# A planned single-core kernel: recurrence, routing and expert tiles, with a new plan, Newton norms and fillers of ones

## The chip, the cores and the metric

The kernel runs on one core of a Trainium2 chip. The metric is the device time of the whole kernel in microseconds, the median over timed runs; the three runs shown of the kernel before have the median 506.29 us (505.67 to 507.88).

## The reference

```python
# x, f_logit: (4, 5056, 256); expert_emb: (8, 256); w1: (8, 256, 1024); w2: (8, 1024, 256)
f = lower_bound + (1 - lower_bound) * sigmoid(f_logit)
for t in range(5056):                       # recurrence along the sequence
    h = f[:, t] * h + (1 - f[:, t]) * x[:, t];  y[:, t] = h
x = y.reshape(20224, 256)
logits = (x / (norm(x) + 1e-6)) @ (expert_emb / (norm(expert_emb) + 1e-6)).T / tau
e = argmax(logits);  gate = softmax(logits)[e]
out = gate * (relu(x @ w1[e]) @ w2[e])      # each token by its one expert
```

## The kernel before

The tokens come in 40 chunks of 512 (the last has 256). For each chunk SyncE loads `f_logit` and `x` (three buffers each); TensorE transposes both (L667, L701); ScalarE makes the gate by tanh (L678, L684); VectorE makes the input term (L709) and runs the recurrence as a scan (L725). ScalarE squares the result (L737). For the first 12 chunks TensorE transposes the result back and ScalarE stores it into `Yt` (L761, L772), later ones go through a bf16 copy and a transposing DMA of SyncE (L743, L748). Two chunks make a group: TensorE computes logits and norms (L819, L823) and ranks the tokens within each expert by triangular matmuls (L887 to L900); some forty short VectorE steps give slot, gate and row. GpSimd then scatters the group's rows, 128 at a time, to the slots of a scratch table in DRAM (`XsScratch`, L1015, 158 scatters).

A tile is 256 slots of one expert. SyncE loads its rows transposed (`ys`, L1207) and its gates and row numbers (`xm`, L1212). TensorE runs 16 matmuls of the first layer (L1247); ScalarE and VectorE evict them by relu into `hT` (L1265, L1270, two buffers). TensorE runs 16 matmuls of the second layer in four steps of four (L1284); ScalarE evicts the first 128 tokens with the gate as scale (L1299), VectorE the others (L1303), into `osb` (four buffers), and GpSimd scatters each half to `out` (L1309, 166 scatters). 83 tiles run here; three more can be needed by the data and are skipped ("late" tiles). All 16 weight arrays are loaded by GpSimd with a cast to bf16 (L647), two at a time, and every tile waits for all of them. A table that `update_` writes after some groups tells which rows a tile reads, so tiles can begin before the last chunk is routed.

What sets the order on each queue is a planner. Each operation is recorded with engine, cost, priority (the chunk number; 10000 + j for tile j; -1 for evictions of tiles and for output scatters), what it reads and writes. `schedule` simulates the five queues with these costs and places, on the engine that can start first, the ready operation of the lowest priority number; banks of PSUM are handed out in the same way (kind "a" for chunks, "m" and "o" for the layers of a tile). The result is a fixed order for each in-order queue, and semaphores carry the dependencies. Two constants tell how scatters and TensorE meet: an end of a TensorE step is planned no earlier than 2500 ns after the start of the last scatter (`SHADOW`), and each scatter waits for the latest TensorE step planned to end 900 ns before the scatter's start (`PACE`), which makes it follow TensorE on the chip too:

```python
if e == "pe": o.end = max(o.end, scat + self.SHADOW)
...
past = [q for t, q in steps[-40:] if t <= s - self.PACE and (o.late or not q.late)]
if past: o.deps.append(past[-1])
```

Of the kernel before, what the change touches and what calls it, by code (L numbers as in the profile page):

```python
# [34 lines left out]
class Prog:  # L35
# [8 lines left out]
    SHADOW = 2500  # L44
    DMA_FIX = 1900
    PACE = 900.0
    DMA_RATE = 400.0

# [65 lines left out]

    def schedule(self, first, caps):
# [24 lines left out]
        bus, scat = 0.0, -1e9  # L140
# [7 lines left out]
        def lag(d):  # L148
            return d.end + self.LAT[d.eng] + self.PAD

# [5 lines left out]
        while True:  # L156
# [16 lines left out]
            if avail[e]:  # L173
                p, i, o = heapq.heappop(avail[e])
            else:
                t, p, i, o = heapq.heappop(wait[e])
            new = [h for h in o.hold if h.b is None]
# [19 lines left out]
            if o.dma is not None:  # L197
                bus = max(bus, free[e]) + o.nbytes / self.DMA_RATE
                o.end = max(bus, free[e]) + self.DMA_FIX
            else:  # L200
                o.end = free[e] + self.LAG[e]
                if e == "pe":
                    o.end = max(o.end, scat + self.SHADOW)
            if e == "pe" and not o.quiet:
                steps.append((free[e], o))
            if e == "pool" and o.dma is not None:
                scat = s
# [121 lines left out]
def bass_hgrn_recurrence__then__cosine_router_kernel(  # L329
# [38 lines left out]
    with ExitStack() as es:  # L368
# [79 lines left out]
        NO = 4  # L448
# [3 lines left out]


        def pool(fn, cost=400, **k):
            return op("pool", fn, cost, **k)
# [12 lines left out]


# [21 lines left out]

        load(0)
        sp(lambda e: e.dma_start(embt[:], moe_expert_emb[:]), 8192, "ld0", w=["embt"])
# [13 lines left out]
        def iota(dst, pattern, base=0, mult=0, w=()):  # L507
# [3 lines left out]

        pool(lambda e: e.memset(ident[:], 0.0), w=["ident"])
# [10 lines left out]
            2, r=["lb0", "lb1"], w=["cs0"],  # L523
# [3 lines left out]
            2, r=["lb0", "lb1"], w=["cs1"],  # L527
# [13 lines left out]
        pool(lambda e: e.memset(onesb[:], 1.0), w=["onesb"])  # L541
# [10 lines left out]
        def late_constants():  # L552
# [54 lines left out]
        dve(lambda e: e.tensor_tensor(ew(3), ew(0), ew(2), ALU.mult), 1, r=["ew0", "ew2"], w=["ew3"])  # L607
        dve(lambda e: e.tensor_tensor(ew(4), ew(1), ew(3), ALU.add), 1, r=["ew1", "ew3"], w=["ew4"])
        dve(
            lambda e: e.tensor_scalar(ew(5), ew(4), 0.5, 1e-6, op0=ALU.mult, op1=ALU.add),  # L610
            1, r=["ew4"], w=["ew5"],
        )
# [20 lines left out]
        )  # L633


        def wload(i, c):
# [9 lines left out]
            op(  # L646
                "pool", lambda e: e.dma_start(dst, src), 1000, w=[("w", i)], dma=f"w{i}",  # L647
                deps=[pr.writer.get(("w", i - 2))], nbytes=1 << 20, prio=c,
            )
# [82 lines left out]
        def Y_(c):  # L732
# [8 lines left out]
            if c >= CT and nb == 4:  # L741
                act(
                    lambda e: e.activation(hbf[c % NHF][:], hb[c % NH][:], AF.Copy),  # L743
                    2 * n, r=[("hb", c % NH, 0), ("hb", c % NH, 1)], w=[("hbf", c % NHF)],
                )
                for dh in range(DT):
                    sp(
                        lambda e, dh=dh: e.dma_start_transpose(  # L748
                            Yt[y][:, gi * 8 + k_ * 4 : gi * 8 + k_ * 4 + 4, dh * P : (dh + 1) * P],
                            hbf[c % NHF][:, dh, :],  # L750
                        ),
                        230000, f"yt{y}_{k_}", r=[("hbf", c % NHF)], w=[("Yt", y, k_, dh)],
                    )
                return
            for hf in range(nb // 2):
# [23 lines left out]
                )  # L779

# [141 lines left out]
        def gate_(bi):  # L922
# [7 lines left out]
            dve(  # L930
                lambda e: e.tensor_scalar(
                    t_.bitcast(I32), n_.bitcast(I32), 1, None, op0=ALU.logical_shift_right
                ),
                16, r=[ki], w=[kt],
            )
            dve(
                lambda e: e.tensor_scalar(
                    y_.bitcast(I32), t_.bitcast(I32), -1.0, 1597463007.0,
                    op0=ALU.mult, op1=ALU.add,
                ),  # L940
                16, r=[kt], w=[ky],
            )
            for _ in range(3):
                dve(
                    lambda e: e.scalar_tensor_tensor(
                        out=t_, in0=y_, scalar=-0.5, in1=y_, op0=ALU.mult, op1=ALU.mult
                    ),
                    16, r=[ky], w=[kt],
                )
                dve(lambda e: e.tensor_tensor(t_, t_, n_, ALU.mult), 16, r=[kt, ki], w=[kt])  # L950
                dve(
                    lambda e: e.scalar_tensor_tensor(
                        out=y_, in0=t_, scalar=1.5, in1=y_, op0=ALU.add, op1=ALU.mult
                    ),
                    16, r=[kt, ky], w=[ky],
                )
# [236 lines left out]

        a1, a2 = {}, {}
        last_mm = {1: None, 2: None}
        EVP = lambda p: -1.0
        OUTP = lambda p: -1.0

        def tile_(j, u, g):
# [78 lines left out]
            ho = Hold("o")  # L1278
            po = lambda s: bank[ho.b][:, s * D : (s + 1) * D]
            for m in range(4):  # L1280
                def mm2(e, m=m):
                    for kf in (2 * m, 2 * m + 1):
                        for s in range(2):
                            i = e.matmul(  # L1284
                                po(s), hT[qh][:, kf, s * P : (s + 1) * P],
                                wall[:, bass.ds(a2[j][kf] - WA, 2 * D)].bitcast(BF16),
                                start=(kf == 0 and s == 0), stop=(kf == FT - 1),
                                skip_group_check=True,
                            )
                    return i  # L1290

                last_mm[2] = pe(
                    mm2, 437, r=[("hT", qh, m)] + [("w", i) for i in range(2 * E)],
                    h=ho, order=[prev],
# [5 lines left out]
                h=ho, r=[("xm", qx)], w=[("osb", qo, 0)], prio=EVP(pr.prio),  # L1300
# [3 lines left out]
                300, h=ho, r=[("xm", qx)], w=[("osb", qo, 1)], prio=EVP(pr.prio),  # L1304
            )
            for s in range(2):
# [15 lines left out]
                sc.paced = True  # L1322
# [38 lines left out]
        NM = NT - 3  # L1361
# [63 lines left out]
```

## Time and profile before

| | |
|---|---|
| median of the runs shown | 506.29 us |
| profiled execution | 503.07 us |
| its span, first to last instruction | 500.9 us |
| TensorE busy | 449.8 us, mean granted clock 0.971 |
| VectorE, ScalarE, GpSimd busy | 371.5, 328.1, 337.1 us |
| tiles' matmuls (L1247, L1284) | 167.1 and 165.5 us |
| scatters (L1309, L1015) | 164.6 and 152.2 us |

A busy share over the whole span mixes three stretches: chunks alone, chunks and tiles together, tiles alone. The profile's 40 slices show where they meet: VectorE's busy tenths fall from 9 to 4 and 5 after some 60% of the span, and TensorE's stay at 9 from there. [...] A row of the chain of waits names what the end was followed back to.

### The profile page before, as it was taken

What the parts mean: (1) busy time and instruction counts of PE and PEld (TensorE: products, weight loads), DVE (VectorE), ACT (ScalarE), POOL (GpSimd) and SP (SyncE); (2) the same over time, 40 slices, a digit from 0 to 9 for tenths busy, and PEclk for the clock granted to TensorE, in tenths of its full rate; (3) what the DMA queues carried; (4) which work ended last, traced back from release to release, by engine and by line L of the source; (5) the groups of instructions that cost most, each with busy time, mean ns of one, the idle gap of its engine ahead of it and who ended that gap; (6) DMA issues with size and microseconds to landing.
All of it is one profiled execution on the core that took longest, in us unless ns stands there. A gap on an engine that the chain in (4) does not pass through costs nothing.

```text
span 500.9 us, 12508 instructions
## 1 busy us (share of the span) xinstructions
PE 449.8 (90%) x4009; PEld 383.7 (77%) x4009; DVE 371.5 (74%) x1202; ACT 328.1 (65%) x549; POOL 337.1 (67%) x404
## 2 busy tenths in 40 slices
PE   4878786587898999999799999999999999999994
PEld 3556564565787877877677688999999999999993
DVE  6799999576998999999899997454545545455552
ACT  6789887466787988988798844444445444454442
POOL 5144376775677677777777777777777777755565
PEclk9989989598998999999999999999999999999999
DMA  8999999789999999999998544656554456645411
GB/s 264 318 299 322 316 314 296 165 193 282 245 241 275 303 262 283 244 297 288 268 306 182 129 109 128 173 131 135 127 139 125 114 129 140 157 120 116 117 34 42
DMA packets 127584, 101.77 MB, mean 203 GB/s; under 512 B 104532, under 2 KB 106591, under 8 KB 127520
## 3 DMA queue, kind: packets, MB, share of 16 engines
q1 hardware_dynamic: 111104, 60.70, 47.2%
q0 software_dynamic: 16416, 40.27, 30.9%
q8 instruction: 34, 0.56, 0.5%
q14 instruction: 30, 0.25, 0.2%
HBM read 58.38 MB, written 34.01 MB: 184 GB/s over the span
## 4 chain that ended last, share of the span: by engine, by line
PE 57%; DVE 19%; DMA 10%; ACT 8%; issue 5%; SPq 1%; POOL 1%; ACTq 0%
PE bank L1247 23%; PE bank L1284 22%; DMA Yt<-hbf 6%; DVE hb L725 5%; PE bank L819 4%; PE bank L667 3%; DVE bank L709 3%; PE bank L701 3%; DVE hT L1270 3%; ACT fg L684 2%; DMA fin<-in_f_logit_dram 2%; ACT th L678 2%; DVE osb L1303 1%; DMA XsScratch<-Yt,sli 1%; ACT sq L737 1%
## 5 line engine op out<-in xcount | busy, mean ns | idle before, releaser
L1309 POOL DMA_INDIRECT out_dram<-osb,xm x166 | 164.6, 991 | 67.2 <-issue 30.5
L1015 POOL DMA_INDIRECT XsScratch<-Yt,sli x158 | 152.2, 963 | 58.9 <-issue 25.4
L1247 PE MATMUL bank<-ys,wall 128*128 128x256 bf16 x1328 | 167.1, 276 | 7.3 <-DMA ys<-XsScratch 5.0
L1284 PE MATMUL bank<-wall,hT 128*128 x1328 | 165.5, 273 | 3.9 <-ACT hT L1265 3.4
L1270 DVE TENSOR_SCALAR hT<-bank 128x512 bf16<-128x512 f32 x166 | 112.7, 685 | 74.9 <-PE bank L1247 72.0
L1247 PEld LDWEIGHTS bank<-ys,wall 128*128 x1328 | 149.1, 144 | 13.4 <-issue 5.6
L1284 PEld LDWEIGHTS bank<-wall,hT 128*128 128x128 bf16 x1328 | 128.5, 98 | 23.0 <-ACT hT L1265 4.2
L1265 ACT ACTIVATE hT<-bank 128x512 bf16<-128x512 f32 x166 | 98.1, 595 | 69.8 <-PE bank L1247 67.9
L725 DVE TENSOR_TENSOR_SCAN hb<-fg,hb,bank 128x512 f32<-128x512 f32 (+4 forms) x78 | 96.4, 1239 | 0.2
L1299 ACT ACTIVATE osb<-bank,xm 128x256 f32<-128x256 f32 x83 | 39.1, 471 | 47.8 <-PE bank L1284 42.3
L701 PE MATMUL bank<-ident,xin 128*128 128x128 f32 x316 | 53.3, 295 | 12.8 <-ACT fg L684 10.4
L684 ACT ACTIVATE fg<-th,cs 128x512 f32<-128x512 f32 (+1 forms) x80 | 64.0, 810 | 1.1
L1303 DVE TENSOR_SCALAR osb<-bank,xm 128x256 f32<-128x256 f32 x83 | 39.7, 478 | 31.8 <-ACT osb L1299 25.2
L709 DVE SCALAR_TENSOR_TENSOR bank<-fg,bank 128x512 f32<-128x512 f32 (+1 forms) x80 | 54.7, 686 | 7.3 <-PE bank L701 5.8
L667 PE MATMUL bank<-ident,fin 128*128 128x128 f32 x316 | 51.9, 294 | 6.4 <-DMA fin<-in_f_logit_dram 5.5
L701 PEld LDWEIGHTS bank<-ident,xin 128*128 128x128 f32 x316 | 38.2, 149 | 23.3 <-ACT fg L684 17.0
L678 ACT ACTIVATE th<-bank 128x512 f32<-128x512 f32 (+1 forms) x80 | 45.7, 587 | 8.0 <-PE bank L667 7.8
L667 PEld LDWEIGHTS bank<-ident,fin 128*128 128x128 f32 x316 | 40.0, 153 | 14.4 <-issue 7.0
L737 ACT ACTIVATE sq<-hb 128x1024 f32<-128x1024 f32 (+1 forms) x40 | 41.8, 1045 | 13.1 <-DVE hb L725 13.0
L819 PE MATMUL bank<-hb,eT 128*8 128x512 f32 (+1 forms) x160 | 41.8, 601 | 6.5 <-ACT th L678 3.3
L823 PE MATMUL bank<-sq,onesf 128*1 128x512 f32 (+1 forms) x160 | 41.7, 600 | 0.0
L743 ACT ACTIVATE hbf<-hb 128x1024 bf16<-128x1024 f32 x27 | 28.3, 1050 | 9.7 <-DMA Yt<-hbf 9.7
(114 smaller groups left out, 301.3 us busy)
## 6 DMA issues: line engine op xcount, KB each, us to landing
fin<-in_f_logit_dram SPq DMA_DIRECT2D x39, 512.0 KB
xin<-in_x_dram SPq DMA_DIRECT2D x39, 512.0 KB
wall<-in_moe_w_dram POOLq DMA_DIRECT2D x16, 512.0 KB, 10.0
out_dram<-osb,xm POOLq DMA_INDIRECT x166
XsScratch<-Yt,sli POOLq DMA_INDIRECT x158
ys<-XsScratch SPq DMA_TRANSPOSE x83
xm<-XsScratch SPq DMA_DIRECT2D x83, 2.0 KB
XsScratch<-nulr SPq DMA_DIRECT2D x8, 136.0 KB
```

The lines of the kernel that those rows point to most:

```text
L667: i = e.transpose(bank[h.b][:, b : nb * P : nb], fin[q][:, b, dh * P : (dh + 1) * P], ident[:],)
L684: lambda e, dh=dh: e.activation(fg[c % 2][:, dh, 0:n], th[dh][:, 0:n], AF.Identity, bias=cs[:, dh, 0:1], scale=cs[:, dh, 1:2],),
L701: i = e.transpose(bank[h.b][:, b : nb * P : nb], xin[q][:, b, dh * P : (dh + 1) * P], ident[:],)
L709: lambda e, dh=dh, h=h: e.scalar_tensor_tensor(out=bank[h.b][:, 0:n], in0=fg[c % 2][:, dh, 0:n], scalar=1.0, in1=bank[h.b][:, 0:n], op0=AL ...
L725: lambda e, dh=dh, s0=s0, s1=s1, init=init, h=h: e.tensor_tensor_scan(hb[c % NH][:, dh, s0:s1], fg[c % 2][:, dh, s0:s1], bank[h.b][:, s0:s ...
L819: i = e.matmul(bank[hl.b][32 * k_ : 32 * k_ + 8, 0:n], eT[:, kt, :], hb[c % NH][:, kt, 0:n], start=(kt == 0), stop=(kt == DT - 1),)
L1015: lambda e, j=o + j, i=o + k_ * 4 + b: e.indirect_dma_start(out=Xs[:, :], out_offset=bass.IndirectOffsetOnAxis(ap=sli[y][:, j : j + 1], axis=0
L1247: i = e.matmul(bank[hh[f // 2].b][:, (f % 2) * T : (f % 2 + 1) * T], wall[:, bass.ds(a1[j][(4 * mp + f) * DT + kt] - WA - WREV, 2 * FT * P ...
L1265: lambda e, o=o, h=h: e.activation(o, bank[h.b][:], AF.Relu), 512,
L1270: lambda e, o=o, h=h: e.tensor_scalar(o, bank[h.b][:], 0.0, None, op0=ALU.max),
L1284: i = e.matmul(po(s), hT[qh][:, kf, s * P : (s + 1) * P], wall[:, bass.ds(a2[j][kf] - WA, 2 * D)].bitcast(BF16), start=(kf == 0 and s == 0 ...
L1309: lambda e, s=s: e.indirect_dma_start(out=out[:, :], out_offset=bass.IndirectOffsetOnAxis(ap=xm[qx][:, s, 1:2], axis=0), in_=osb[qo][:, s, :],
```

## The change

- The planner loses `SHADOW`; `PACE` becomes 0, so a scatter waits for the latest TensorE step planned to have ended. GpSimd's short operations are planned at 250 ns instead of 400, a weight load's issue at 700 instead of 1000.
- When VectorE would take an operation of more than 400 ns, the planner looks 250 ns ahead for one of higher rank with priority 1 or lower (evictions of tiles, the head's constants) and takes that first.
- Where the planned TensorE sits idle for over 900 ns, a filler is put into its queue: n matmuls of ones, 128x128 by 512 columns, into a free bank, so many that they fill the gap but 350 ns. It depends on the ones only, and on the last reader of its bank.
- The priority of output scatter j becomes 10 + j/2 instead of -1. `osb` has six buffers instead of four. Scatters of the last four regular tiles and of the late ones don't wait for a TensorE step.
- The norms of the embeddings come from a shift, a multiply-add and three Newton steps on VectorE instead of ScalarE's square root and a correction; the router's Newton steps are the same function with two factors in another order. These operations rank among the clears of the banks. The embedding load is issued ahead of chunk 0, the ones and the gate's constants come earlier.
- The back-transposes of chunk c rank as c + 0.4.
- In the last regular tile the second layer runs the first 128 tokens in full and then the others, in two banks, so that the first half can be evicted earlier.

```diff
-    SHADOW = 2500
-    PACE = 900.0
+    PACE = 0.0
+    UNIT = 215.0
+    IDLE = 900.0
+    REST = 350.0
+    COLD = 12000.0
...
+    def filler(self, q, n):
+        f = Op()
+        f.eng, f.dma, f.nbytes, f.cost = "pe", None, 0, n * self.UNIT
...
+        f.deps, f.order = [self.warm_on], []
+        f.fn = lambda e: self.warm(e, q, n)
...
+            if e == "dve" and avail[e] and avail[e][0][2].cost > 400:
+                soon = min(
+                    (w for w in wait[e] if w[0] <= s + 250 and w[1] < avail[e][0][0] and w[1] <= 1),
+                    default=None, key=lambda w: w[:3],
+                )
...
+            gap = s - free[e]
+            if e == "pe" and not o.late and gap > self.IDLE:
+                room = [(t, q) for q, t in enumerate(frees) if t is not None and t <= s - self.IDLE]
+                if room and ready_at(self.warm_on) is not None:
+                    t, q = min(room)
+                    a = max(t, free[e], ready_at(self.warm_on))
+                    n = int((s - a - self.REST) / (self.UNIT * (2 if s < self.COLD else 1)))
+                    if n > 0:
+                        f = self.filler(q, n)
...
+                        if banks[q][1].eng != e:
+                            f.deps.append(banks[q][1])
...
-                if e == "pe":
-                    o.end = max(o.end, scat + self.SHADOW)
...
-        NO = 4
+        NO = 6
...
+        def warm(e, q, n):
+            for _ in range(n):
+                i = e.matmul(
+                    bank[q][:].rearrange("p (a b) -> p a b", a=4), onesb[:],
+                    onesb[:].unsqueeze(1).to_broadcast([P, 4, P]), start=True, stop=True,
+                )
+            return i
...
-        def pool(fn, cost=400, **k):
+        def pool(fn, cost=250, **k):
...
+        def newton(n_, y_, t_, kn, ky, kt, cols):
+            dve(
+                lambda e: e.tensor_scalar(
+                    t_.bitcast(I32), n_.bitcast(I32), 1, None, op0=ALU.logical_shift_right
+                ),
...
...
+            for _ in range(3):
+                dve(lambda e: e.tensor_tensor(t_, y_, n_, ALU.mult), cols, r=[ky] + kn, w=[kt])
...
+        sp(lambda e: e.dma_start(embt[:], moe_expert_emb[:]), 8192, "ld0", w=["embt"])
         load(0)
-        sp(lambda e: e.dma_start(embt[:], moe_expert_emb[:]), 8192, "ld0", w=["embt"])
...
+        pr.warm_on = pool(lambda e: e.memset(onesb[:], 1.0), w=["onesb"])
...
+        pr.prio = -1.75
-        act(lambda e: e.activation(ew(1), ew(0), AF.Sqrt), 1300, r=["ew0"], w=["ew1"])
-        dve(lambda e: e.reciprocal(ew(2), ew(1)), 1, r=["ew1"], w=["ew2"])
...
+        newton(ew(0), ew(1), ew(2), ["ew0"], "ew1", "ew2", 1)
+        dve(lambda e: e.tensor_tensor(ew(3), ew(0), ew(1), ALU.mult), 1, r=["ew0", "ew1"], w=["ew3"])
...
-        OUTP = lambda p: -1.0
+        OUTP = lambda p: 10 + (p - 10000) * 0.5
...
+            split = j == NM - 1
+            ho = [Hold("o"), Hold("o")] if split else [Hold("o")] * 2
...
+                if split:
+                    at = [(kf, m // 2) for kf in range(4 * (m % 2), 4 * (m % 2) + 4)]
...
-                sc.paced = True
+                sc.paced = j < NM - 4
```

## Rows read from the trace of the kernel before

**Rows 1.** page of the profile, header and part 1 (busy time, share, instructions).

```profile
span 500.9 us, 12508 instructions
...
PE 449.8 (90%) x4009; PEld 383.7 (77%) x4009; DVE 371.5 (74%) x1202; ACT 328.1 (65%) x549; POOL 337.1 (67%) x404
```

**Rows 2.** busy us by stretch (instructions): TensorE, weight loads, VectorE, ScalarE, GpSimd; clock, DMA.

```profile
0.00:94.00 94.00, 66.17 (x519) 48.46 (x520) 81.26 (x296) 73.05 (x116) 47.48 (x94) 0.92 1.01 293
94.00:308.00 214.00, 197.63 (x1791) 159.54 (x1791) 195.13 (x744) 165.91 (x273) 156.00 (x172) 0.97 0.97 237
308.00:494.00 186.00, 185.96 (x1703) 175.74 (x1700) 94.65 (x161) 88.65 (x160) 129.77 (x137) 1.00 0.49 124
...
430.00:494.00 64.00, 63.96 (x586) 60.26 (x584) 31.80 (x55) 30.01 (x54) 37.25 (x39) 1.00 0.40 99
```

**Rows 3.** chain of waits in order of time: start us, us, what.

```profile
83.54 5.43 DMA XsScratch<-Yt,sli
...
93.86 3.60 PE bank L1247 x16
...
364.71 3.49 PE bank L1284 x32
```

**Rows 4.** waits of SyncE's queue: line, releaser, us in total, times, longest.

```profile
SPq L306 <- DMA XsScratch<-Yt,sli: 9.7, 1, 9.7
```

**Rows 5.** the weight tile: its loads (ns min/median/max, first to last), landing.

```profile
L647 POOL DMA_DIRECT2D wall<-in_moe_w_dram x16: 528/648/902, 4.2 to 84.5; - x16
...
DMA to landing us min/median/max: 7.0/10.0/14.8
```

**Rows 6.** groups by line: times run, busy us, mean ns of one, idle before.

```profile
L1309 POOL DMA_INDIRECT out_dram<-osb,xm x166 | 164.6, 991 | 67.2 <-issue 30.5 <-ACT hT L1265 11.5 <-DVE hT L1270 9.0
L1015 POOL DMA_INDIRECT XsScratch<-Yt,sli x158 | 152.2, 963 | 58.9 <-issue 25.4 <-PE bank L701 7.0 <-PE bank L823 4.1
...
L950 DVE TENSOR_TENSOR nr<-nr,nrm 128x8 f32<-128x8 f32 (+2 forms) x66 | 10.4, 157 | 0.4
```

**Rows 7.** timeline of the tail: start us, us, instruction, idle before it.

```profile
488.81 0.47 ACT L1299 ACTIVATE osb<-bank,xm 128x256 f32<-128x256 f32 x1 [0.33 <-PE bank L1284]
...
491.12 0.47 DVE L1303 TENSOR_SCALAR osb<-bank,xm 128x256 f32<-128x256 f32 x1
...
491.32 0.98 POOL L1309 DMA_INDIRECT out_dram<-osb,xm  x1 [2.53 <-ACT hT L1265]
...
492.05 1.91 PE L1284 MATMUL bank<-wall,hT 128*128 x16
...
494.05 0.47 ACT L1299 ACTIVATE osb<-bank,xm 128x256 f32<-128x256 f32 x1 [1.20 <-PE bank L1284]
...
497.76 0.99 POOL L1309 DMA_INDIRECT out_dram<-osb,xm  x1 [0.30 <-issue]
```

**Rows 8.** busy us by stretch, routing scatters of line 1015 alone (GpSimd, clock, DMA).

```profile
0.00:94.00 94.00, 29.51 (x31) 0.92 1.01 293
```

**Rows 9.** timeline of ScalarE at the head: start us, us, instruction.

```profile
8.62 1.28 ACT L605 ACT_TABLE_LOAD   x1
...
11.42 1.08 ACT L678 ACTIVATE th<-bank 128x512 f32<-128x512 f32 x2
```

**Rows 10.** waits, whole span: engine, line, releaser, us in total, times, longest.

```profile
DVE osb L1303 <- DMA out_dram<-osb,xm: 5.6, 4, 1.9
...
PE bank L1247 <- DMA ys<-XsScratch: 5.0, 1, 5.0
...
PE bank L1284 <- ACT hT L1265: 3.4, 3, 1.8
```

**Rows 11.** busy us in stretches of 4 us (columns as in rows 2).

```profile
88.00:92.00 4.00, 0.83 (x4) 0.42 (x2) 3.77 (x7) 2.40 (x4) 3.09 (x4) 0.50 0.67 151
92.00:96.00 4.00, 2.15 (x11) 1.70 (x12) 0.21 (x1) 0.21 (x1) 3.07 (x5) 0.50 0.78 133
...
120.00:124.00 4.00, 4.00 (x25) 1.85 (x18) 0.74 (x5) 3.36 (x7) 1.11 (x2) 0.57 1.50 289
```

More of the change, by code (lines that the diff above doesn't have):

```diff
@@ L149, in lag, with ready_at @@
             return d.end + self.LAT[d.eng] + self.PAD
+        def ready_at(d):
+            return lag(d) if hasattr(d, "end") else None
         def unpark(t):
@@ L172, in schedule @@
             s, e = best
-            if avail[e]:
+            soon = None
+            if e == "dve" and avail[e] and avail[e][0][2].cost > 400:
[3 more added lines that the diff above has]
+                )
+            if soon is not None:
+                wait[e].remove(soon)
+                heapq.heapify(wait[e])
+                s, p, i, o = soon
+            elif avail[e]:
                 p, i, o = heapq.heappop(avail[e])
@@ L176, in schedule @@
                 t, p, i, o = heapq.heappop(wait[e])
+            gap = s - free[e]
[7 more added lines that the diff above has]
+                        f = self.filler(q, n)
+                        f.start = a
+                        free[e] = a + n * self.UNIT * (2 if s < self.COLD else 1)
+                        f.end = free[e] + self.LAG[e]
+                        if banks[q][1].eng != e:
+                            f.deps.append(banks[q][1])
+                        banks[q][1], frees[q] = f, free[e]
+                        out.append(f)
             new = [h for h in o.hold if h.b is None]
@@ L633, in bass_hgrn_recurrence__then__cosine_router_kernel @@
         )
+        pr.prio = 0
         def wload(i, c):
@@ L754, in Y_ @@
                 return
+            pr.prio = c + 0.4
             for hf in range(nb // 2):
@@ L779, in Y_ @@
                 )
+            pr.prio = c
         def views(g, hr=None):
@@ L929, in gate_ @@
             ki, ky, kt = ("nrm", q), ("nr2", q), ("nr3", q)
[L930 to L956, printed above, removed]
+            newton(n_, y_, t_, [ki], ky, kt, 16)
             dve(
@@ L1192, in addresses @@
             ]
+        NM = NT - 3
         a1, a2 = {}, {}
@@ L1277, in tile_, with po, mm2 @@
             prev.quiet = True
-            ho = Hold("o")
-            po = lambda s: bank[ho.b][:, s * D : (s + 1) * D]
+            split = j == NM - 1
+            ho = [Hold("o"), Hold("o")] if split else [Hold("o")] * 2
+            def po(s):
+                return bank[ho[s].b][:, 0:D] if split else bank[ho[s].b][:, s * D : (s + 1) * D]
             for m in range(4):
[L1281 to L1289, printed above, removed]
+                if split:
+                    at = [(kf, m // 2) for kf in range(4 * (m % 2), 4 * (m % 2) + 4)]
+                else:
+                    at = [(kf, s) for kf in (2 * m, 2 * m + 1) for s in range(2)]
+                def mm2(e, at=at):
+                    for kf, s in at:
+                        i = e.matmul(
+                            po(s), hT[qh][:, kf, s * P : (s + 1) * P],
+                            wall[:, bass.ds(a2[j][kf] - WA, 2 * D)].bitcast(BF16),
+                            start=(kf == 0 and (s == 0 or split)), stop=(kf == FT - 1),
+                            skip_group_check=True,
+                        )
                     return i
                 last_mm[2] = pe(
-                    mm2, 437, r=[("hT", qh, m)] + [("w", i) for i in range(2 * E)],
-                    h=ho, order=[prev],
+                    mm2, 437, r=[("hT", qh, kf // 2) for kf, s in at[::2]] + [("w", i) for i in range(2 * E)],
+                    h=ho[at[0][1]], order=[prev, last_mm[2] if m else None],
                 )
```

48 lines of the change are left out of this document (33 added, 15 removed).

## The prediction

> **What bounds the kernel now.** I read the page's header first: the span is 500.9 us, TensorE is busy for 449.8 of it [rows 1]. Then the busy time by stretch, cut at the first expert tile (94 us) and at the last routed group (308 us) [rows 2]. The three stretches have three limits. From 0 to 94 us there is no expert tile yet: TensorE works 66.17 of 94 us, the DMA engines' share is 1.01 and VectorE is at 81.26. From 94 to 308 chunks and tiles are mixed: VectorE 195.13 of 214, TensorE 197.63, at a granted clock of 0.97. From 308 to 494 only tiles are left, and TensorE is busy for 185.96 of 186 us. So the end is set by the sum of TensorE's work, and every microsecond that TensorE idles or runs slow after the first tile comes back at the end.
>
> The chain of waits shows the size of that work: 32 second-layer matmuls in 3.49 us, 0.109 each, so 32 x 0.109 = 3.49 us a tile, and 83 tiles are 290 us [rows 3]. It also shows why tiles begin at 94: a routing scatter issued at 83.54 takes 5.43 us to land, the tile's first load follows, and the first matmuls start at 93.86. SyncE's queue stood 9.7 us at that scatter with the chunk loads behind it [rows 4], and the last weight load is issued only at 84.5, with a median of 10.0 us to landing [rows 5]. Weights, scatters and chunk loads share a full DMA, so I don't expect the first tile much before 94.
>
> What can be recovered from 94 on: 214 - 197.63 = 16.4 us of idle TensorE, and about 0.03 x 214 = 6.4 us of clock [rows 2]; at most 23 us. GpSimd sets a second floor. Its scatters take 0.99 us (output, 166 of them) and 0.96 (routing, 158) [rows 6], and 0.30 lies between two that run back to back [rows 7]. 31 routing scatters are done by 94 us [rows 8]; the rest is 166 x 1.29 + 127 x 1.26 = 374 us, so from 94 it can't be done before 468, against 498.8 now. The gain can't exceed some 30 us by that floor.
>
> **The change part by part.** I sum against the profiled execution: 503.07 us, which is 2.2 around the span of 500.9. The median of the runs shown, 506.29, lies 3.2 above it, and I add that at the end.
>
> *Norms by Newton steps, loads and constants moved.* In the first chunk ScalarE loads a table at 8.62, does the one square root, loads the first table again, and goes on with tanh at 11.42: 2.80 us go [rows 9]. They lie on the chain of waits. [...] In their place VectorE gets 13 short steps instead of 4 (a shift, a multiply-add, three times three, two more), and the 9 more are 1.4 us at 0.157 each, as in the router's own Newton steps [rows 6]; they now rank among the bank memsets, so DVE can stand at the embedding load with the clears of banks 3 to 7 behind it, and TensorE's first transposes of chunk 1 wait for those banks: between 0 and 3 us against. The embedding load goes ahead of chunk 0 on SyncE's queue (one issue, under half a microsecond). How much of the 2.80 reaches 94 us? The DMA is full there, so between 0 and 2.8; I take 1.0 less, nearer to the hidden end.
>
> *Plan without the shadow, cheaper GpSimd costs, look-ahead on VectorE, Y transposes ranked later.* No instruction is added; the order on each queue changes. Before, the plan took every TensorE step's end as at least 2.5 us after the last scatter's issue, so each eviction was planned late and banks were held long. The trace shows no such delay: in the tail the last matmuls end at 492.05 + 1.91 = 493.96, scatters run there back to back, and ScalarE's eviction begins at 494.05 [rows 7]. The idle 16.4 us is the price of orders that did not fit. Named waits there: 5.0 us for the first tile's load, 3.4 us for ScalarE's hT [rows 10]. Bounds: all 16.4 back, or as much again lost, since a tight plan has no slack for a late eviction. I take 6 less, about a third: the 5.0 for the first tile's load stays, because only landing ends it.
>
> *Ranked output scatters, six output buffers, scatters wait for the latest TensorE step.* Output scatter j now ranks as chunk 10 + j/2, no longer ahead of all. Routing scatters of old chunks go first, outputs lag, and six buffers cover it. VectorE waited 5.6 us for an output buffer [rows 10]; that goes, but most of it is under TensorE's full stretch: nothing counted. The wait: formerly for a step planned to end 0.9 us before, now for the latest. Behind a waiting scatter stand all later ones; routing scatters gate the next tile loads, output scatters gate the buffers and through them the evictions. Cost: from 430 to 494 GpSimd has 64 - 39 x 1.29 = 13.7 us to spare [rows 2, 6], so up to 13.7 us of waits are hidden, and I take 0. With 293 scatters after 94, 0.05 us each uses the cover up.
>
> *Fillers of ones.* A filler matmul has 512 columns, two of the 256-column ones at 0.109, so 0.218 at full clock [rows 3]; in the first tile, at half clock, 16 took 3.60 us, so 0.45. They stand in TensorE's queue where the plan sees over 0.9 us of idle. They cost nothing where the machine idles too, and all they take where it is late by then. Bounds for the displacement: 0 to 16.4 us (as much as idles there now); I take 1 more, since most planned gaps should lie before 94. [...] Of 6.4 us I take 2 less, bounds 0 and 6.4. [...]
>
> *The tail.* At the end six output scatters run back to back from 491.32, 1.29 apart, to the last at 497.76. The first of them stood idle 2.53 us, although its data were ready at 488.81 + 0.47 = 489.28 [rows 7]. The last four tiles no longer wait for a step. From 489.4 at 1.29 apart the last starts at 495.9, 1.9 less; but the second one's data come from VectorE at 491.12 + 0.47, which gives 491.7 + 4 x 1.29 = 496.9, 0.9 less. The split last tile has its first half evicted 0.87 earlier, which keeps up with that. I take 1.5 less, bounds 0 and 2.8.
>
> Sum: -1.0 - 6 + 1 - 2 - 1.5 = -9.5. 503.07 - 9.5 = 493.6 for a profiled run, and with the 3.2 the median is 496.8.
>
> **Rivals.**
> 1. *Much of the idle goes* (0.20). The tight plan recovers 14 of the 16.4 and 5 of the clock, head and tail give 2.5: 21.5 less, 485. For it: VectorE's and TensorE's sums both fit into 94 to 308. Against: VectorE is at 195 of 214 there.
> 2. *No change* (0.15). DMA hides the head, idle only moves, fillers take what the clock gives: the tail's 1.5 is left, 504.8. For it: the first tile is fixed by landings.
> 3. *Slower: TensorE waits for evictions* (0.17). Place: the second-layer matmuls behind hT, four steps a tile, two hT buffers. Without the 2.5 us of margin the order puts them right behind the eviction, which on VectorE is longer than planned. From 308 on there is no idle now [rows 2], with some 53 tiles: 0.2 us a tile are 10.6 and cancel the gain; that is the point from which it decides. At 0.5 us a tile it is 26.5 - 9.5 = 17 more, 523; at 0.3, 512. Against: hT costs 3.4 us in the whole span today [rows 10].
> 4. *Slower: GpSimd becomes the bound* (0.08). If the new waits average 0.1 us on 293 scatters, 29 - 13.7 = 16 come out at the end, less 9.5: 513. Against: it runs nearly back to back, so each scatter already starts later than the step that it waits for. For it: from 94 to 308 its busy 156.00 us and some 160 gaps of 0.30 (172 instructions, a dozen of them iotas) are 204 of 214 us, no room to catch up in [rows 2].
>
> **How the numbers follow.** The forecast has 0.40, its own range being 489 to 502. A measurement tells 0.5%, 2.5 us, from no change. Faster: 0.40 + 0.20 = 0.60; same 0.15; slower 0.17 + 0.08 = 0.25. The range takes in rival 1 with room to 480 and the rivals 3 and 4 up to 511, where about 0.1 lies on each side.
>
> **What would show it.** Right: idle from the first tile to 494 clearly under 16.4; clock over 0.98 there; no ScalarE table load but the first; fillers before 94 mostly; the last scatter some 3 us after TensorE's end instead of 4. Wrong: idle before second-layer matmuls in the tile-only stretch, filler time inside full stretches, GpSimd without slack at the end, or the first tile later than 94.

## The result, and the profile after

The changed kernel takes 490.55 us (median of five runs, 489.50 to 494.20) against 506.28 (504.40 to 507.88) for the kernel before: a ratio of 0.9706, 95% interval 0.967 to 0.9741, or 15.7 us less. The forecast was 496.8 in a range of 480 to 511.

The first page of the changed kernel, header and busy times, against [rows 1]:

```profile
span 492.4 us, 12545 instructions
...
PE 459.8 (93%) x4075; PEld 383.7 (78%) x4075; DVE 371.0 (75%) x1211; ACT 325.5 (66%) x546; POOL 337.9 (69%) x404
```

The span fell by 8.5 us although TensorE is busy 10 us more. The extra is the fillers, which are one line of the view by line (count, first and last start, ns):

```profile
L494 PE MATMUL bank<-onesb x66: 377/379/634, 1.5 to 485.4; 128*128 128x512 bf16 x66
```

66 of them in 18.1 us; 64 stand before 94 us and two at 485.2, so no full stretch pays for them. Without them TensorE is busy 441.7 us for the same 4009 matmuls, 8.1 less than before.

Busy time by stretch of the changed kernel (columns as in [rows 2]):

```profile
0.00:94.00 94.00, 81.41 (x618) 51.50 (x618) 85.90 (x304) 75.53 (x120) 49.00 (x95) 1.00 1.03 294
94.00:308.00 214.00, 199.60 (x1827) 164.39 (x1828) 188.76 (x683) 165.12 (x272) 152.68 (x167) 0.97 1.01 241
308.00:494.00 186.00, 178.80 (x1632) 167.81 (x1630) 96.31 (x225) 84.82 (x155) 136.27 (x143) 0.99 0.52 121
```

By 94 us 618 - 64 = 554 real matmuls are done against 519, and the granted clock, a share of TensorE's full speed, is 1.00 instead of 0.92. From 94 to 308 TensorE idles 214 - 199.60 = 14.4 us instead of 16.4. What is left for the last stretch is 1632 - 2 = 1630 matmuls against 1703: 73 fewer, 8.0 us at 0.109. Of these, 6.6 us arrive (TensorE's last matmul ends at 487.34 instead of 493.96, see the tail below), and with the tail's 1.9 they are the 8.5 of the span.

Where the head was won is seen in its last 14 us. First the kernel before, then the changed one, from 80 to 94 us:

```profile
80.00:94.00 14.00, 5.89 (x47) 4.28 (x40) 11.36 (x52) 8.08 (x13) 10.45 (x13) 0.72 0.89 229
```

```profile
80.00:94.00 14.00, 11.52 (x94) 6.24 (x93) 13.66 (x44) 13.62 (x21) 10.48 (x13) 1.00 1.09 271
```

47 matmuls before, 94 now, of which 7 are fillers. Before, the first tile's matmuls stood early in TensorE's queue, with too little in front of them to fill the time until their load lands [rows 10, 11]. The new plan puts 36 more matmuls ahead of the first tile, 554 instead of 518 (fillers not counted): 20 transposes and 16 for logits and norms. TensorE in the changed kernel, start, us, and in brackets the wait before:

```profile
91.60 0.59 PE L900 MATMUL bank<-sq,onesf 128*1 128x512 f32 x1
...
96.12 1.07 PE L1299 MATMUL bank<-ys,wall 128*128 128x256 bf16 x8 [3.50 <-DMA ys<-XsScratch]
```

The first tile now begins at 96.12 instead of 93.86 [rows 3], at a granted clock of 1.00 from 96 to 100 us, against 0.50 from 92 to 96 before [rows 11] (8 matmuls in 1.07 us, before 16 in 3.60), and the stand ahead of it is 3.5 instead of 5.0. It is later and costs less, since work that had to be done anyway came first.

The tail of the changed kernel, against [rows 7]:

```profile
485.87 1.47 PE L1344 MATMUL bank<-wall,hT 128*128 x12
486.55 0.47 ACT L1359 ACTIVATE osb<-bank,xm 128x256 f32<-128x256 f32 x1 [1.00 <-PE bank L1344]
...
487.43 0.48 DVE L1363 TENSOR_SCALAR osb<-bank,xm 128x256 f32<-128x256 f32 x1 [1.71 <-issue]
487.98 0.98 POOL L1369 DMA_INDIRECT out_dram<-osb,xm  x1 [0.30 <-DVE osb L1363]
489.26 0.98 POOL L1369 DMA_INDIRECT out_dram<-osb,xm  x1 [0.30 <-DMA out_dram<-osb,xm]
```

TensorE ends at 485.87 + 1.47 = 487.34 and the last scatter starts 1.92 us later; before it was 497.76 - 493.96 = 3.80. The tail gives 1.9.

At the head ScalarE loads one table only. Between gate and tanh, where the table loads took 2.80 us [rows 9], it now waits 1.37 us for TensorE's transposes, and the tanh begins at 10.99 instead of 11.42:

```profile
0.75 1.28 ACT L753 ACT_TABLE_LOAD   x1 [0.75 <-PEq L1466]
...
8.09 1.52 ACT L759 ACTIVATE fg<-th,cs 128x512 f32<-128x512 f32 x2 [0.39 <-DVE embw L536]
10.99 1.08 ACT L753 ACTIVATE th<-bank 128x512 f32<-128x512 f32 x2 [1.37 <-PE bank L742]
```

Yet the first transposes of `x` begin at 8.96 instead of 7.95. They follow the gate, and the gate follows two constants that VectorE makes from `lower_bound` (`lbt`). That load lands 1.0 us later than before, which VectorE waits for (first the kernel before, then the changed one):

```profile
6.73 0.17 DVE L522 TENSOR_SCALAR cs<-lbt 128x2 f32<-128x2 f32 x1 [1.53 <-DMA lbt<-in_lower_bound_dram]
```

```profile
7.73 0.24 DVE L601 TENSOR_SCALAR cs<-lbt 128x2 f32<-128x2 f32 x1 [2.33 <-DMA lbt<-in_lower_bound_dram]
```

The load is issued at nearly the same time (2.60 instead of 2.50); why it lands later is not shown. The transposes of chunk 0's `f_logit`, whose load now stands behind the embedding's, begin at 5.12 instead of 4.46.

GpSimd's scatters, times run, busy us, mean ns, idle before them, against [rows 6]:

```profile
L1369 POOL DMA_INDIRECT out_dram<-osb,xm x166 | 164.7, 992 | 58.3 <-issue 29.2 <-ACT hT L1317 6.5 <-PE bank L1299 4.9
L1066 POOL DMA_INDIRECT XsScratch<-Yt,sli x158 | 152.3, 964 | 60.1 <-issue 23.2 <-PE bank L776 10.5 <-PE bank L1299 6.3
```

118.4 us of idle in front of scatters against 126.1: the later wait did not add any.

### The profile page after: what moved, and what is told of

The parts are those of the page before. It is cut to its first block, busy times and chain, and to the rows that moved or that the text cites. A ratio compares the mean times of both kernels' runs of the same rounds, so it can differ in the third digit from the quotient of the medians.

```text
span 492.4 us, 12545 instructions
## 1 busy us (share of the span) xinstructions
PE 459.8 (93%) x4075; PEld 383.7 (78%) x4075; DVE 371.0 (75%) x1211; ACT 325.5 (66%) x546; POOL 337.9 (69%) x404
## 4 chain that ended last, share of the span: by engine, by line
PE 72%; DMA 11%; ACT 10%; SPq 3%; issue 2%; DVE 1%; POOL 0%; ACTq 0%; POOLq 0%; DVEq 0%
PE bank L1344 27%; PE bank L1299 27%; PE bank L896 6%; PE bank L776 5%; PE bank L742 4%; DMA Yt<-hbf 3%; ACT fg L759 3%; DMA xin<-in_x_dram 3%; ACT th L753 2%; DMA ys<-XsScratch 2%; ACT sq L812 1%; DMA XsScratch<-Yt,sli 1%; PE bank L837 1%; SPq L1259 1%; DMA lbt<-in_lower_bound_dram 1%
## 5 line engine op out<-in xcount | busy, mean ns | idle before, releaser
L1344 PE MATMUL bank<-wall,hT 128*128 x1328 | 176.5, 275 | 10.6 <-ACT hT L1317 6.6
L1299 PE MATMUL bank<-ys,wall 128*128 128x256 bf16 x1328 | 173.1, 274 | 4.2 <-DMA ys<-XsScratch 3.5
L776 PE MATMUL bank<-ident,xin 128*128 128x128 f32 x316 | 50.5, 283 | 8.6 <-ACT fg L759 4.6
L776 PEld LDWEIGHTS bank<-ident,xin 128*128 128x128 f32 x316 | 36.4, 144 | 19.7 <-ACT fg L759 11.6
L742 PE MATMUL bank<-ident,fin 128*128 128x128 f32 x316 | 49.0, 281 | 1.8 <-DVE embw L536 1.3
L742 PEld LDWEIGHTS bank<-ident,fin 128*128 128x128 f32 x316 | 37.1, 144 | 10.5 <-issue 3.8
L818 ACT ACTIVATE hbf<-hb 128x1024 bf16<-128x1024 f32 x27 | 28.4, 1052 | 14.4 <-DMA Yt<-hbf 14.4
```

Of the source, the lines that this page charges most:

```text
L742: i = e.transpose(bank[h.b][:, b : nb * P : nb], fin[q][:, b, dh * P : (dh + 1) * P], ident[:],)
L776: i = e.transpose(bank[h.b][:, b : nb * P : nb], xin[q][:, b, dh * P : (dh + 1) * P], ident[:],)
L1299: i = e.matmul(bank[hh[f // 2].b][:, (f % 2) * T : (f % 2 + 1) * T], wall[:, bass.ds(a1[j][(4 * mp + f) * DT + kt] - WA - WREV, 2 * FT * P ...
L1344: i = e.matmul(po(s), hT[qh][:, kf, s * P : (s + 1) * P], wall[:, bass.ds(a2[j][kf] - WA, 2 * D)].bitcast(BF16), start=(kf == 0 and (s == ...
```

## The experiments

The kernel was changed in one place at a time. Two kinds have to be kept apart: with some edits the plan stays the same, instruction for instruction (fillers thinned, waits taken away or moved); others are planned anew, and then the whole order moves. They ran on three chips: e1 to e4 on one, e5 to e8 on a second, e9 to e12 on a third. On the second and the third the kernel before has the same median, 506.54.

**Fillers thinned, in the changed kernel's own order (e1).**

```diff
-            for _ in range(n):
-                i = e.matmul(bank[q][:]..., start=True, stop=True)
+            return e.matmul(bank[q][:, 0:8], onesb[:], onesb[:, 0:8], start=True, stop=True)
```

> The changed kernel in its own order, each filler group cut to one matmul of 8 columns. The heat theory (fillers pay by keeping TensorE's clock up around the first tiles): clock under 0.95 before 96 us as in the kernel before, the first tile's 16 matmuls at half rate again, and 3 to 6 us slower than the changed kernel, near 495. The plan theory (the order brings most, fillers 2 us less 1 displaced): within 2 us of it, 489 to 493. The displacement theory (fillers stand in late work's way): faster, 486 to 489.

Measured 583.57 us, ratio 0.9962 (0.9938 to 0.9985). On this chip the kernel before takes 585.71 (median of 17 runs, 581.91 to 591.12), 79 us more than on the others, and the changed kernel itself was not run there. So the four runs on it are read against each other and not against 490.55.

**No scatter waits for a TensorE step, in the changed kernel's own order (e2).**

```diff
-                sc.paced = j < NM - 4
+                sc.paced = False
```

(the same for the routing scatters)

> The changed kernel in its own order, no scatter waits for a TensorE step. The plan theory, with these waits hidden: within 1.5 us of the changed kernel, 489 to 492. The theory that the later wait costs GpSimd (rival 4 of the prediction): 3 us or more faster. The theory that the wait is what helps, by keeping scatters off TensorE's and ScalarE's loads: 3 us or more slower, 494 and up.

Measured 650.04 us, 1.1134 (1.1087 to 1.118): 66 us above the run before it, whose waits are there (and whose fillers are thinned). ScalarE's waits for the first layer's matmuls that the profile can put down to no instruction ("remote"; us in total, times, longest), first in e1, then in this run, and a place in its tile stretch:

```profile
ACT hT L1312 <- remote: 15.2, 6, 4.4
```

```profile
ACT hT L1317 <- remote: 54.6, 12, 7.2
```

```profile
502.20 1.04 PE L1299 MATMUL bank<-ys,wall 128*128 128x256 bf16 x8
503.39 1.00 POOL L1369 DMA_INDIRECT out_dram<-osb,xm  x1 [0.30 <-issue]
504.00 0.60 ACT L1317 ACTIVATE hT<-bank 128x512 bf16<-128x512 f32 x1 [2.33 <-PE bank L1299]
504.00 0.69 DVE L1322 TENSOR_SCALAR hT<-bank 128x512 bf16<-128x512 f32 x1 [1.81 <-PE bank L1299]
```

The matmuls end at 502.20 + 1.04 = 503.24, a scatter is issued at 503.39, and both evictions start only at 504.00, 0.76 later. In the changed kernel's tail, on a chip where the kernel before takes 506.28, ScalarE's and VectorE's evictions follow TensorE's ends within some 0.1 us (484.13 after 484.04, 487.43 after 487.34), and its waits list nothing "remote". So on the slower chip ScalarE has such waits even where the scatters wait for TensorE (15.2 us in e1), and more of them where they don't (54.6). There the scatters' waits are worth some 66 us. Why this chip does so is not shown.

**The shadow of 2500 ns back in the plan; and the old rank with four buffers (e3 and e4).**

```diff
+                if e == "pe":
+                    o.end = max(o.end, scat + self.SHADOW)
```

```diff
-        NO = 6
-        OUTP = lambda p: 10 + (p - 10000) * 0.5
+        NO = 4
+        OUTP = lambda p: -1.0
```

> The changed kernel with the 2500 ns shadow back in the plan, so another order on all queues. The plan theory: the 6 us that I gave to the order come back, 495 to 498. The theory that order hardly matters: within 1.5 us of the changed kernel. Rival 3 (a plan without margin lets TensorE wait for evictions): faster, under 489.

> The changed kernel with output scatters ranked ahead of all again (-1) and four output buffers. The plan theory, which counted nothing for ranks and buffers: 489 to 492. The theory that ranking brings tiles earlier: output scatters delay routing scatters again, fewer tiles done at 308 us, 3 to 8 us slower, 494 to 498.

Measured 592.42 (1.0114, 1.0077 to 1.0152) and 590.98 (1.0102, 1.007 to 1.0134) on the same chip as the two above, 1.5 and 1.3% above the thinned kernel. Both were planned anew, and after what follows I read no price of a single edit from them; only that neither old setting, planned in this way, is better there.

**The changed kernel again, on another chip (e5).** No edit.

> The changed kernel once more, as the anchor for kernels that run beside it. The first four experiments ran where the kernel before takes 585.7 us instead of 506 and where TensorE's semaphores reach ScalarE and VectorE late around scatters. If the gain is one of the plan alone, the ratio is 0.97 wherever it runs. If the lost shadow and the tighter wait matter where semaphores come late, the ratio there is 0.99 or above; if the later wait is what protects TensorE's signals, it is 0.97 or below there too.

Measured 491.58 us, 0.971 (0.9676 to 0.9743), the kernel before 506.54. Its stretches:

```profile
0.00:94.00 94.00, 80.69 (x618) 51.42 (x618) 85.55 (x304) 75.75 (x120) 49.84 (x96) 1.00 1.03 294
94.00:308.00 214.00, 201.66 (x1857) 166.09 (x1858) 192.75 (x706) 166.49 (x274) 153.49 (x168) 0.98 1.00 242
308.00:494.00 186.00, 175.52 (x1602) 164.62 (x1600) 93.38 (x202) 83.25 (x153) 134.31 (x141) 0.99 0.50 120
```

Span 489.9 us; 1602 - 2 = 1600 matmuls are left at 308, 103 fewer than before. The profiled execution took 491.66, close to its kernel's median.

**A plan with 10% more margin (e6).** A control: nothing of the change is taken out, only the order moves.

```diff
-    PAD = 100
+    PAD = 110
```

> Control for chance: the changed kernel with the planner's margin PAD at 110 ns instead of 100, which makes another order of about the same quality. If orders of one quality scatter little, within 0.5% of the changed kernel beside it; if an order's details are worth as much as the edits, 1% or more either way, and then single edits that re-plan can't be told apart by one run each.

Measured 503.61 us, 0.9934 (0.989 to 0.9978). Nearly the whole gain is gone. TensorE in this kernel:

```profile
111.95 1.90 PE L1299 MATMUL bank<-ys,wall 128*128 128x256 bf16 x8 [14.83 <-DMA ys<-XsScratch]
```

One stand of 14.83 us, where the changed kernel has 3.50 (and 2.53 in e5). SyncE's queue (start, us on the queue) shows what was issued ahead of the tile's load:

```profile
83.75 9.27 SPq L823 DMA_TRANSPOSE Yt<-hbf  x2
94.36 3.65 SPq L1259 DMA_TRANSPOSE ys<-XsScratch  x1
...
99.83 6.94 SPq L1259 DMA_TRANSPOSE ys<-XsScratch  x1
```

A pair of transposing DMAs for chunk 12's `Yt` at 83.75, and only then the first tile's transposing load at 94.36, which takes 111.95 - 94.36 = 17.6 us until TensorE has it. In the changed kernel it was issued at 88.29 and used at 96.12, 7.8 us.

**The kernel before without shadow and without the 900 ns (e7).**

```diff
-    PACE = 900.0
+    PACE = 0.0
-                    o.end = max(o.end, scat + self.SHADOW)
+                    pass
```

> The kernel before with the shadow off and the wait on the latest TensorE step (PACE 0), nothing else. The plan theory, in which the order brings 6 of 9.5 us: ratio to before about 0.988. Rival 3 (no margin): 1.00 to 1.03. The theory that the later wait protects the signals where they come late: 0.97 or below where the kernel before takes 585 us, about 0.99 where it takes 506.

Measured 521.72 us, 1.0283 (1.0237 to 1.0328), the slowest of this chip. It has the pair of transposing DMAs ahead of the first tile too (82.78, tile's load at 90.43, used at 111.20), and there TensorE's long stand is for a chunk's `x`, 11.35 us; for the tile's rows it waits 1.95 only. Then it has a second long stand. TensorE, and SyncE's wait that goes with the second:

```profile
104.38 1.09 PE L701 MATMUL bank<-ident,xin 128*128 128x128 f32 x4 [11.35 <-DMA xin<-in_x_dram]
...
111.20 1.90 PE L1247 MATMUL bank<-ys,wall 128*128 128x256 bf16 x8 [1.95 <-DMA ys<-XsScratch]
...
436.73 4.86 PE L1247 MATMUL bank<-ys,wall 128*128 128x256 bf16 x24 [18.92 <-DMA ys<-XsScratch]
```

```profile
SPq L306 <- DMA XsScratch<-Yt,sli: 28.4, 2, 27.1
```

From 417.8 TensorE stands 18.9 us for a tile's rows, whose load stands behind a routing scatter on SyncE's queue; from 406 to 430 GpSimd runs routing scatters one at a time (406.44, 410.29, 416.74, 420.59, 424.44) between output scatters, which rank first here. So taking the margin alone loses 15 us in this kernel, with both stands in it. That the old rank and the shadow belong together would explain it, and is not tested.

**The square root back on ScalarE (e8).**

```diff
-        newton(ew(0), ew(1), ew(2), ["ew0"], "ew1", "ew2", 1)
+        act(lambda e: e.activation(ew(1), ew(0), AF.Sqrt), 1300, r=["ew0"], w=["ew1"])
```

(and the old correction steps)

> The changed kernel with ScalarE's square root back (its two table loads and the old correction). My sum took 1.0 us for it, bounds 0 to 2.8: 0 to 0.6% slower than the changed kernel beside it. The theory that the head is on the path in full: 2.8 us, 0.6%; more than 1% would be the order's doing.

Measured 499.07 us, 0.9868 (0.9832 to 0.9904). By the trace the square root is not the reason: in the new order it runs at 3.81, before the first gate is there, and the second table load ends at 4.03 + 1.28 = 5.31, 0.6 us ahead of the first tanh. The plan moved, and again the transposing DMAs came ahead of the tile's load:

```profile
82.62 3.01 SPq L828 DMA_TRANSPOSE Yt<-hbf  x2
88.14 4.69 SPq L1264 DMA_TRANSPOSE ys<-XsScratch  x1
...
94.20 8.09 SPq L1264 DMA_TRANSPOSE ys<-XsScratch  x1
```

```profile
109.24 3.32 PE L1304 MATMUL bank<-ys,wall 128*128 128x256 bf16 x16 [14.57 <-DMA ys<-XsScratch]
```

From 88.14 to 109.24 are 21.1 us.

On the chips where the kernel before takes 506, three of three kernels with that pair ahead of the tile's load stand over 11 us there, none without it. One run takes the pair away.

**More margin as in e6, chunk 12's `Yt` made on TensorE (e10).**

```diff
-    PAD = 100
-        CT = 12
+    PAD = 110
+        CT = 13
```

> The changed kernel with PAD 110 as in e6, and chunk 12's Yt made on TensorE (CT 13) instead of by two transposing DMAs, which in e6 stood on SyncE's queue at 83.75 us, ahead of the first tile's load. Jam theory: with no transposing DMA ahead of the first ys load the DMA engines move 160 to 280 GB/s between 92 and 104 us (e6: 112, 142, 91), the first tile's load lands within 9 us of its issue, TensorE stands under 5 us there (e6: 14.8), and 12 us come back less about 1.2 us for two more groups of transposes on TensorE: 490 to 495 us. Rival (the padded plan is the worse order whatever that chunk does): 500 to 505 us, with a stand of 10 us or more at the first tile or elsewhere.

Measured 492.00 us, 0.9709 (0.9653 to 0.9765): 11.6 of the 12.0 us are back. SyncE and TensorE:

```profile
89.09 1.40 SPq L1259 DMA_TRANSPOSE ys<-XsScratch  x1
...
91.85 3.37 SPq L1259 DMA_TRANSPOSE ys<-XsScratch  x1
...
105.36 3.40 SPq L823 DMA_TRANSPOSE Yt<-hbf  x2
```

```profile
99.80 1.90 PE L1299 MATMUL bank<-ys,wall 128*128 128x256 bf16 x8 [3.59 <-DMA ys<-XsScratch]
```

The stand is 3.59 us as expected; the load took 99.80 - 89.09 = 10.7 us, not the 9 that I allowed. Busy time in steps of 4 us, first e6, then this kernel (last two numbers: DMA share, GB/s):

```profile
100.00:104.00 4.00, 0.00 (x0) 0.00 (x0) 0.00 (x0) 0.00 (x0) 3.04 (x4) 0.60 1.42 91
104.00:108.00 4.00, 0.00 (x0) 0.00 (x0) 0.00 (x0) 0.00 (x0) 0.98 (x1) 0.50 1.22 71
```

```profile
100.00:104.00 4.00, 4.00 (x34) 3.63 (x33) 1.69 (x5) 2.15 (x3) 3.08 (x4) 0.66 1.03 208
104.00:108.00 4.00, 3.53 (x32) 1.59 (x29) 3.73 (x11) 3.08 (x5) 2.57 (x5) 1.00 0.98 139
```

With the early pair the DMA engines are busier than over e6's first 94 us (1.42 and 1.22 against 1.06) and move 91 and 71 GB/s; without it 208 and 139. From 92 to 104 us, for which 160 to 280 was expected, the new kernel moves 208, 152 and 208, e6 112, 142 and 91. So the slow transfers go when the pair goes. This was done in one kernel of three, and its plan was made anew, so other things moved with it; what makes the packets slow is not shown. In the changed kernel the DMA engines move 352 GB/s in all from 112 to 116 us, with such a pair issued at 111.52 beside chunk loads, so a pair alone did not make them slow there.

**The thinned fillers once more, where the kernel before takes 506.54 (e9).** The edit is that of the first run.

> The changed kernel in its own order, each group of fillers cut to one matmul of 8 columns. Clock theory (the gain is that the same 4009 matmuls run at full clock because the fillers keep TensorE at work): the granted clock before 94 us falls back from 1.00 to about 0.92, TensorE's busy time without fillers goes back from 440 to 442 us to 446 to 449 us, and the time is 496 to 499 us (0.979 to 0.986 of the kernel before). Order theory (the new plan took idle time away): the order is the same, so the time stays at 490 to 493 us.

Measured 494.30 us, 0.9746 (0.9703 to 0.9788). Its stretches:

```profile
0.00:94.00 94.00, 71.77 (x537) 53.16 (x538) 80.51 (x292) 70.35 (x112) 49.64 (x95) 0.91 1.02 291
94.00:308.00 214.00, 202.86 (x1855) 165.29 (x1853) 194.72 (x697) 171.09 (x280) 151.86 (x167) 0.98 1.04 242
308.00:494.00 186.00, 178.76 (x1635) 168.18 (x1633) 96.88 (x225) 85.34 (x156) 136.48 (x144) 0.99 0.50 122
```

The clock before 94 falls to 0.91, as expected, and the matmuls done by then to 537 - 12 = 525, 29 fewer than with fillers: 3.2 us. The first tile begins at 98.68, and TensorE does not stand for its load:

```profile
98.68 1.09 PE L1294 MATMUL bank<-ys,wall 128*128 128x256 bf16 x8
```

By 308 us the 29 are no longer to be seen: 1635 - 1 = 1634 matmuls are left, against 1630, 1600 and 1650 in the three traces with full fillers in this order (the changed kernel's two and e12's). The time lies between both theories: by the medians the kernel is 2.4 to 3.8 us slower than the three sets of runs with fillers in this order (490.55, 491.58, 491.89). Only the last of them is from this chip, and there the runs overlap (492.03 to 495.40 against 488.14 to 495.21), so the price of the fillers is likely and not shown.

The same thinned kernel has the ratio 0.9962 on the first chip (e1) and 0.9746 here: most of its gain does not come on the first chip.

**The kernel before with the fillers alone (e11).** The code of the fillers in the kernel before, planned with its shadow, pace and ranks; its first tile's load comes ahead of the first transposing DMA.

```diff
+            gap = s - free[e]
+            if e == "pe" and not o.late and gap > self.IDLE:
...
+                        f = self.filler(q, n)
```

> The kernel before with the fillers alone (its plan made again with them; pace, shadow, ranks, square root and tail as before; its first load for a tile comes ahead of the first transposing DMA, as in the kernel before). Clock theory: the granted clock before 94 us rises from 0.92 to 0.98 or more, TensorE's busy time without fillers falls from 450 us to 442 to 445 us, time 497 to 501 us (0.982 to 0.99). Order theory (fillers fill gaps that were idle anyway and win nothing): 504 to 508 us.

Measured 507.08 us, 1.0006 (0.9975 to 1.0038): nothing. From 0 to 94 and from 80 to 94 us:

```profile
0.00:94.00 94.00, 80.91 (x602) 52.48 (x602) 81.60 (x296) 72.74 (x116) 47.03 (x93) 0.98 1.00 293
```

```profile
80.00:94.00 14.00, 8.96 (x70) 4.96 (x62) 12.22 (x52) 8.13 (x14) 10.44 (x13) 1.00 0.93 242
```

The clock rises to 0.98 and no more is done. My clock theory, which had read the 8.1 us of lower busy time as the gain, falls with this run: 84 fillers raised the clock, 602 - 84 = 518 real matmuls are done by 94 us against 519, and what TensorE saved it stood idle. Over the whole span it is busy 464.5 - 25.6 = 438.9 us without fillers, 10.9 less than in the kernel before, and the time is the same.

**The scatters wait for an earlier step again, in the changed kernel's own order (e12).**

```diff
-    PACE = 0.0
+    PACE = 900.0
```

> The changed kernel in its own order, each paced scatter waiting for a TensorE step that the plan ends 900 ns earlier, as in the kernel before, instead of the latest one. If the later wait costs GpSimd nothing and wins TensorE nothing here: 489 to 493 us, the same as the changed kernel. If the later wait is what keeps scatters off TensorE's steps: slower, 495 us or more, with longer stands of TensorE for hT. If the later wait held GpSimd up: 486 to 488 us.

Measured 491.89 us, 0.9691 (0.9643 to 0.9739): the same as the changed kernel. Which step a scatter waits for doesn't matter here. Two of its stretches, for the comparison of traces below:

```profile
94.00:308.00 214.00, 198.25 (x1808) 161.88 (x1809) 187.19 (x668) 164.58 (x271) 150.65 (x164) 0.98 1.02 240
308.00:494.00 186.00, 180.26 (x1652) 170.00 (x1649) 98.80 (x240) 85.91 (x157) 137.29 (x144) 1.00 0.50 123
```

A run without any such wait was made only on the first chip.

## Why the prediction was right, and where its sizes were off

| step of the sum | forecast | found |
|---|---|---|
| head: norms, loads, constants | -1.0 | no run shows it alone; ScalarE's next tanh 0.4 earlier, the first transposes of `x` 1.0 later |
| fillers: clock -2, displaced +1 | -1 | -3.2 by 94 us; nothing left at 308 in the traces; -2.4 to -3.8 by the medians |
| order of the plan, idle from 94 to 308 | -6 | -2.0 and -4.0 in the two traces of the changed kernel, -0.6 in e12, -5.2 in e9 |
| wait, rank, buffers | 0 | wait 0 by e12; rank and buffers not separable |
| tail | -1.5 | -1.9 |
| from the profiled execution to the median | +3.2 | -0.1 in e5, -3.6 in the first profile |

*The head.* The table loads are gone, but of their 2.80 us only 0.43 is seen at ScalarE's next tanh, and the first transposes of `x` come 1.0 later. So no gain of the head by itself is seen in the traces; e8, which puts the square root back, was planned anew and does not price it either.

*The order.* The place was partly right. The 5.0 us for the first tile's load were to stay, "because only landing ends it". That step failed as put: landing ends the stand, but the order decides how much work lies in front of it, and 40 more real matmuls went there (80 to 94 us). So a part of the order's gain lies before 94 us, where I had looked for none. Order and fillers can be told apart there by what stands ahead of the first tile: 554 real matmuls in the new order, with full fillers and with thinned ones, and 518 in the old order, without fillers and with them (e11). The fillers only move the time at which these are done: in the new order the first tile begins between 94.49 and 96.12 with them and at 98.68 without. From 94 to 308 the idle is less by 0.6 to 5.2 us in the four traces of the new order, all short of the 6, and one trace does not settle the size.

What makes the order better is not shown. The forecast took the idle for the price of the shadow. The kernel before without it is 15 us slower (e7), and the run with the shadow back was planned anew, on the chip where evictions come late (e3, with 12.4 us of "remote" waits ahead of ScalarE's hT). Which of the edits to the plan brings the gain stays open.

*The fillers* were undersized, if the medians are right. The sum counts 2 us of clock for them from 94 on, and no run shows that term: "clock over 0.98 there" did not come, the two traces of the changed kernel have 0.97 and 0.98 from 94 to 308, with 0.97 before. What the runs show is the clock before 94 us, 1.00 against 0.92. The 7.5 us of lost clock there, an estimate (0.08 x 94 [rows 2]), had no place in the sum. In the old order that is right, as e11 shows (clock 0.98, ratio 1.0006). In the new order TensorE has work in front of the first tile, and that tile began later where the clock before 94 us was 0.91 (98.68 in e9) than where it was 1.00 (94.49 to 96.12); how much of it reaches the end the traces leave open. "Fillers before 94 mostly" came.

*The offset.* Half of the 6.2 us by which the median was missed. I added 3.2 us because the kernel before's profiled execution lay that far below its median, as if that were a property of the code around the span. Of 28 later runs of that kernel on two chips one is below 503.07: the traced execution lies at the low end of that kernel's runs. The changed kernel's second profiled execution lies close to its median. Without the offset the forecast would have been 493.6, 3.1 above what came. It also limits what traces can tell: the pairs of traces show 8.5 and 11.0 us of the span, the medians 15.7 and 15.0. The other 4 to 7 us belong to executions that were not traced, and stay open: the kernel before's trace lies 3.2 under its median, and the changed kernel's first one 3.6 over its own.

*The rivals.* Much of the idle goes (485): no, of the 16.4 us at most 5.2 came back. No change (504.8) is out. TensorE behind its evictions: not here, the stretch of tiles is as full as before (308 to 450 us: 141.55 of 142, before 142.00), but the four runs on the first chip look like it, with second-layer matmuls waiting 33.8 us for hT in e1; whether the kernel before waits as long there, no trace shows. GpSimd as the bound: e12 and the scatters' idle time speak against it here. "The first tile later than 94" was named as a sign against the forecast; it came, and was none.

**What moves this kernel most is none of the steps.** The pair of transposing DMAs sits ahead of the first tile's load in e6, e7 and e8 (17.6, 20.8 and 21.1 us from the load's issue to its use), and not in the kernel before, the changed kernel, e9, e10, e11 and e12 (3.9 to 10.7). A tenth more margin is enough to flip it, and it costs 12 us, more than the whole forecast of 9.5. Nothing in the code keeps the kernel before and the changed one on the good side. That the forecast came out was to that extent luck: the same change with a margin of 110 takes 503.61, close to "no change".

## What to carry over

Where a planner writes the queues, one edit moves everything: compare by a control that changes the order only, look for what flipped in it (here two DMAs ahead of one load) and run with that taken away, before any edit is given a price. A higher clock or a filled gap won nothing where TensorE's time was not the limit (e11: clock before 94 us 0.98 instead of 0.92, ratio 1.0006); ask of the order where that is before counting it. One profiled execution lay 3.2 us under its kernel's median, another 3.6 over; such a distance is no term to carry to another kernel.

## What was not expected of the hardware

- One chip runs these kernels slower, the kernel before by 79 us (585.71 against 506.54) and the thinned one by 89 (583.57 against 494.30), at the same granted clock (0.971 profiled in e1 and in e9). There the scatters' waits for TensorE are worth some 66 us (e2).
- In e6 the DMA engines were busy throughout and moved far less than before for 16 us: 112, 142, 91 and 71 GB/s from 92 to 108, with 0.95 to 1.42 of share, against 304 over its first 94 us.
- With the fillers of ones the granted clock before 94 us was 1.00 (the changed kernel, e5), with thinned ones 0.91 (e9), although the fillers run 18.1 us in all; in the old order it was 0.98 with them (e11) and 0.92 without.
